# First v blocks ahead of the second q/k chunk, earlier masks, held sinks, later v: a reordering in a planned attention and MLP kernel

## The chip, the core and the metric

The kernel runs on one core of one Trainium2 chip. Its time is the device time in microseconds (us) of one execution; the figure quoted for a kernel is the median of several runs. TensorE does the matmuls, VectorE (DVE), ScalarE (ACT) and GpSimd (POOL) the elementwise work, and SyncE (SP) only issues transfers. POOL issues the loads that convert from float32 to bfloat16, SP the DMA transposes and the stores.

## What is computed

Sliding-window attention with sinks, then layer norm and an MLP with a residual. The reference, cut to what matters:

```python
# q, k, v: (4, 8, 768, 64); n_sink 4, window 128
scores = scale * np.matmul(q, k.transpose(0, 1, 3, 2))
is_sink = pos[None, :] < n_sink
rel = pos[:, None] - pos[None, :]
keep = is_sink | ((rel >= 0) & (rel < window))
a = softmax(np.where(keep, scores, -1e9))
x = matmul(a, v)                        # heads joined: (4, 768, 512)
xn = (x - mu) / np.sqrt(var + 1e-06) * g_ln
out = x + np.maximum(xn @ w_ch1, 0.0) @ w_ch2   # 512 -> 2048 -> 512
```

## The kernel before

**Tiles.** The 4 x 768 rows are 24 tiles of 128 rows, numbered t = 6b + r for row block r of batch b. A tile is attended by `scores` (L472), exp on ScalarE (L509), a mask, and `values` (L544). A block of 128 keys meets its own 128 queries and the next 128, so one set of scores is 64x128 by 64x256 matmuls (L498) in two halves of four heads, each half in one of two PSUM buffers `pw`. For the first four tiles the mask is added on TensorE (L494, from neg0 and neg1); for the others it is multiplied afterwards, on VectorE (L513, L519) or POOL (L521, L524). `values` multiplies by v with an extra column of ones (L565, L568), adds the sinks (L558, from row block 2 on), and empties the `pw` buffer on VectorE: reciprocal L590, product L592 (xt), statistics L598 and L601, centred and multiplied by g L606 (xn). xn is transposed on TensorE (L645), from tile 12 on by a DMA transpose (L635).

**Sinks.** Keys 0 to 3 of a batch reach every row. `sinks` (L426) makes masked copies of the sink keys (ks, L434, on VectorE, from the transposed k), spreads the sink values (L444 on TensorE, L449 on VectorE), multiplies all later queries by the sink keys (L457) and takes the exp (es, L462).

**MLP.** Tiles are in groups of 2, 2, 2, 4, 4, 4, 4, 2. `up` (L658) does 4 matmuls with w_ch1 (L666) and a relu on ScalarE or VectorE (L675, L677), 16 times per group; `down` (L685) does 16 matmuls with w_ch2 (L697) per tile, then L710 and the store L715. For the first three groups all ups come ahead of all downs. The reciprocal standard deviation of a group is made on POOL (L618 ve, L620 rs) from its tiles' statistics.

**Loads.** All loads of q, k, v and the weights are issued by POOL in one chain; at most eight are outstanding, as the trace shows. Batch 0's q and k come in two chunks of 384 rows (the first in two halves of heads), batch 1's in one (`load_runs`, L303), and both are transposed on TensorE (L386, `prep_runs`) and copied to qkt by ScalarE or VectorE (L182, L184). Batches 2 and 3 are loaded by row block (`load_qk`, L327) and transposed by DMA on SP (`prep`, L409). v is loaded by row block (`load_v`, L336).

**Order.** Nothing is scheduled at run time: each engine runs its own list in order. The list is made when the program is built. Every step is an `op` with its engines, an assumed cost, a key (its due time) and its dependencies. `Plan.emit` (L54) keeps a clock for each engine, takes the engine that can start first, and among the ops that could start there within a small slack the one of the lowest key. `LAT` (L37) is what is assumed between the end of an op and its use by another engine: 2.0 for a load, 0.7 for a DMA transpose. Ahead of each TensorE op before 26 us of that clock it puts dummy matmuls (`spin`, L192) into the gap it foresees (L104 to L109). The assumed costs therefore decide which instruction stands where, and a wait that was foreseen wrongly holds up all that stands behind it on its engine. The steps that the prediction follows are L434 on VectorE, the loads L312, L336 and L327 and the selects L242 and L244 on POOL, and L386, L494, L498, L558, L565, L666 and L697 on TensorE.

Of the kernel before, what the change touches and what calls it, by code (L numbers as in the profile page):

```python
# [31 lines left out]
class Plan:  # L32
# [10 lines left out]
    WARM = 26.0  # L43
    AHEAD = 2.5

    def __init__(self, spin):
        self.ops, self.spin = [], spin

    def op(self, engs, fn, deps=(), key=0.0, alloc=(), uses=()):
        o = Op(engs, fn, deps, key, alloc, uses)  # L50
        self.ops.append(o)
        return o

    def emit(self):  # L54
# [3 lines left out]
        def ready(o):  # L58

            r, held = 0.0, False  # L60
            for d in o.deps:
                if d.end is None:
                    return None, False

                r = max(r, d.end - (self.LAT[d.eng] - 0.03 if len(o.engs) == 1 and d.eng in o.engs else 0.0))
            n = {}
            for b in o.alloc:
                h = hist.get(b.pool, [])
                k = n[b.pool] = n.get(b.pool, -1) + 1
                if len(h) + k >= b.bufs:  # L70
                    for u in h[k - b.bufs].users:
                        if u.end is not None:
                            r = max(r, u.end)
                        elif b.pool == "pw":
                            held = True
                        else:
                            return None, False
            return (None if held else r), held

        trace = []  # L80
        while waiting:
# [7 lines left out]
            for o in waiting:  # L89
                r = at[o]  # L90
                if r is None:
                    continue
                if any(b.pool == "pw" for b in o.alloc) and any(o.key > k and max(r, free.get("PE", 0.0)) > a for k, a in pairs):
                    continue
                e, c = min(o.engs.items(), key=lambda x: max(r, free.get(x[0], 0.0)) + x[1] + (
                    self.SPARE.get(x[0], 0.0) if len(o.engs) > 1 else 0.0))
                s = max(r, free.get(e, 0.0))
# [6 lines left out]
            if e == "PE" and s < self.WARM:  # L104
                f = max(free.get(e, 0.0), 1.3)
                n = int((min(s, 5.0) - f) / 0.107) if f < 5.0 else 0
                n += int((s - max(f, 5.0) - 0.1) / 0.057) if s > 5.0 else 0
                for _ in range(n if s < 7.0 else n // 2):
                    self.spin()  # L109
            free[e] = s + c  # L110
            o.end, o.eng = s + c + self.LAT[e], e
            for b in o.alloc:
# [9 lines left out]
def kernel(  # L122
# [12 lines left out]
    nc = tc.nc  # L135
# [138 lines left out]
    ident_done = op({"POOL": 0.35}, const_ident, [begun], -499.5)  # L274
    half_masks = op({"POOL": 0.7}, const_masks, [begun], -488)
    masks_done = neg_done = op({"DVE": 0.8}, const_negs, [half_masks], -495)
    sinks_done = op({"POOL": 1.4}, const_sinks, [begun], -440)
# [24 lines left out]

    def load_runs(b, c, x, h0, h1, key):  # L303
        alloc = qn_buf(b, x)
# [9 lines left out]

        o = load(0.6 + 0.04 * (h1 - h0), (h1 - h0) * w * 256 / 390e3, go, key, (), alloc, [qb])
        for h in range(h0, h1):
            loaded[(b, c, x, h)] = o

    def load_qk(b, x, r, key, deps=()):
# [8 lines left out]

        o = load(0.9, 0.92, go, key, deps, alloc, [qb])
        prep(b, x, r, o, key)  # L330
# [3 lines left out]
    def load_v(b, r, key, deps=()):  # L334
# [4 lines left out]
        before = [vread[(b - 2, i)] for i in (r, r + 1) if (b - 2, i) in vread] + [vs_done.get(b - 2)]  # L339
        vcast[(b, r)] = load(0.9, 0.92, go, key, list(deps) + before)  # L340

# [59 lines left out]
    def prep(b, x, r, lo, key):  # L401
# [9 lines left out]
        o = op({"SP": 1.25}, go, [lo], key, alloc, [kb, qb])  # L411
        prepped[(b, r, x)] = op({"XD": 0.4}, None, [o], key, (), [kb, qb])

# [9 lines left out]

    sunk, esb = {}, {}

    def sinks(b, key):  # L426
# [36 lines left out]

        o1 = op({"DVE": 0.2}, mul_k, ready(b, range(HP), 0, NS, 0, 0) + [sunk.get(b - 2), sinks_done], key, (), [kb])
        ov = op({"PE": 0.22}, mm_v, [vcast[(b, 0)], sinks_done, ones_done], key, [vb])
# [3 lines left out]

    ebuf, edone = {}, {}  # L470

# [72 lines left out]
    def values(t, key):  # L544
# [89 lines left out]
        if t >= DMA_TILE:  # L634
            o = op({"SP": 1.25}, lambda _: nc.sync.dma_start_transpose(room(), xnb[t].t), [o], key, alloc,  # L635
                   [xnb[t], xtb[g]])
            turned[t] = op({"XD": 0.4}, None, [o], key, (), [xnb[t], xtb[g]])
            return
# [97 lines left out]

    gb_done = op({"PE": 1.0}, spread_g, [op({"SP": 5.2}, None, key=-1000)], -600, [gp])
    gb_done = op({"ACT": 0.6}, lambda _: nc.scalar.copy(gb, gp.t), [gb_done], -600, (), [gp])

    for half in range(2):  # L740
        for x in range(2):
            load_runs(0, 0, x, 4 * half, 4 * half + 4, -500 + half)
    for x in range(2):
        load_runs(0, 1, x, 0, H, -491 + x)
    for r in range(3):
        load_v(0, r, -486 + r)
    for c in range(4):
        load_w(1, c, -470 + 2 * c)
        if c < 3:
            load_v(0, 3 + c, -469 + 2 * c)  # L750
    for c in range(3):
        load_w(2, c, -440 + c)
    for x in range(2):
        load_runs(1, 0, x, 0, H, -436 + x)
    load_w(2, 3, -434)
# [3 lines left out]
    for b in range(B):  # L759
        k0 = bkey[b]  # L760
        if b == 0:
            for c in range(2):
                for hp in range(HP):
                    prep_runs(0, c, hp, k0 + (0.6 if c else -40) + 0.1 * hp)
                if c == 0:
# [19 lines left out]
        else:  # L785
# [3 lines left out]
            for r in range(RB):  # L789
                load_v(b, r, k0 - 50 + r)  # L790
        sinks(b, akey(RB * b + 2) - 6)
        for r in range(RB):
            attention(RB * b + r, akey(RB * b + r))

    for s, g in mlp_order:
# [48 lines left out]
```

## Time and profile before

| | |
|---|---|
| time, median of 13 runs | 237.33 us (236.5 to 243.31) |
| profiled execution: time | 237.33 us |
| profiled execution: span, mean granted clock | 235.6 us, 0.978 |
| TensorE busy | 224.0 us, of which up (L666) 88.5, down (L697) 57.9 + 31.7 |
| VectorE, ScalarE, POOL busy | 113.8, 116.2, 79.6 us |
| chain that ended last | TensorE 83%, DMA 6%, VectorE 5% |
| loads | 24.93 MB moved, mean 106 GB/s; batch 1's k: 768 KB, 20.9 us from issue to landing |
| DMA transposes of q and k (24) | 8.1 us from issue to landing |

How to read it. The span runs from the first to the last instruction of the profiled execution; the time has a little more around it. A row of the timeline gives the start, the duration, the engine, the line and the operation, output <- inputs, and in brackets how long the engine was idle before and what ended that. "xN" joins N instructions. A row of the windows gives for each engine the busy time in the stretch and the number of instructions, then the granted TensorE clock as a share of full speed, the DMA engines' share and GB/s. Releasers are inferred; where the engine named had long been done, it was something else, often a DMA.

### The profile page before, as it was taken

How to read it: one execution, taken by the hardware profiler on the slowest of the kernel's cores; microseconds unless marked ns; L12 is line 12 of the kernel's file. 1: busy time of each engine (PE TensorE's matmuls, PEld its weight loads, DVE VectorE, ACT ScalarE, POOL GpSimd, SP SyncE). 2: the span in 40 equal slices, each digit the busy share in tenths (PEclk: the TensorE clock that was granted, in tenths of full speed). 3: DMA queues.
4: the chain of work that ended last, by engine and by line, in shares of the span. 5: the costliest groups of instructions: out<-in, count | busy, mean ns of one | idle time of the engine just before them, and what ended most of it. 6: DMA issues, size and time to landing. Idle time of an engine off the chain costs nothing.

```text
span 235.6 us, 4404 instructions
## 1 busy us (share of the span) xinstructions
PE 224.0 (95%) x1808; PEld 123.3 (52%) x1808; DVE 113.8 (48%) x211; ACT 116.2 (49%) x188; POOL 79.6 (34%) x106
## 2 busy tenths in 40 slices
PE   8798999989879999999999999999999999999993
PEld 6344678876425455544555444454445554444851
DVE  1328578058476879856648445753007570021011
ACT  2467787879323553787123864316633147500820
POOL 7958663569716777530020300202004120000000
PEclk9679999999979999999999999999999999999999
DMA  6999999999999999999132101212002221012102
GB/s 70 152 180 191 199 206 205 200 157 154 127 154 163 168 207 156 181 159 168 58 93 88 22 3 24 93 67 67 0 1 69 90 67 25 0 45 89 47 0 89
DMA packets 83478, 24.93 MB, mean 106 GB/s; under 512 B 74241, under 2 KB 80385, under 8 KB 83458
## 3 DMA queue, kind: packets, MB, share of 16 engines
q0 software_dynamic: 60416, 13.64, 68.5%
q1 hardware_dynamic: 23040, 11.02, 22.6%
q8 instruction: 14, 0.23, 0.4%
q14 instruction: 6, 0.05, 0.1%
q10 hardware_dynamic: 2, 0.00, 0.0%
HBM read 27.27 MB, written 6.29 MB: 142 GB/s over the span
## 4 chain that ended last, share of the span: by engine, by line
PE 83%; DMA 6%; DVE 5%; ACT 2%; issue 1%; POOL 1%; SPq 0%; POOLq 0%; DVEq 0%; ACTq 0%
PE pm L697 35%; PE pm L666 32%; PE pw L498 5%; DMA qkt<-qkn 3%; PE pw L565 2%; DMA qkn<-in_k_dram 2%; PE pw L494 2%; PE pw L568 2%; PE pw L558 1%; DVE qkt L184 1%; DVE xt L592 1%; POOL qkn L312 1%; ACT e L509 1%; PE bank L645 1%; PE pm L386 1%
## 5 line engine op out<-in xcount | busy, mean ns | idle before, releaser
L666 PE MATMUL pm<-xnt,w1s 128*128 128x256 bf16 (+1 forms) x512 | 88.5, 326 | 0.0
L509 ACT ACTIVATE e<-pw 128x1024 bf16<-128x1024 f32 x44 | 43.7, 1024 | 49.5 <-PE pw L498 49.5
L666 PEld LDWEIGHTS <-w1s 128*128 128x128 bf16 x512 | 48.4, 98 | 33.3 <-issue 2.3
L697 PE MATMUL pm<-w2s,h1t 128*128 128x512 bf16 x256 | 57.9, 379 | 0.0
L710 DVE SCALAR_TENSOR_TENSOR ot<-pm,rs,xt 128x512 f32<-128x512 f32 x24 | 18.0, 748 | 64.2 <-PE pm L697 46.9
L675 ACT ACTIVATE h1t<-pm 128x512 bf16<-128x512 f32 x60 | 35.8, 597 | 21.9 <-PE pm L666 21.9
L697 PEld LDWEIGHTS <-h1t 128*128 128x128 bf16 x256 | 24.1, 98 | 28.2 <-issue 0.8
L697 PE MATMUL pm<-w2s,h1n 128*128 128x512 bf16 x128 | 31.7, 391 | 0.0
L675 ACT ACTIVATE h1n<-pm 128x256 bf16<-128x256 f32 x57 | 21.2, 389 | 17.6 <-PE pm L666 15.2
L336 POOL DMA_DIRECT2D vn<-in_v_dram x24 | 21.4, 896 | 4.7 <-DMA qkn<-in_q_dram 1.4
L521 POOL TENSOR_SCALAR_AFFINE_SELECT e<-e 128x512 bf16<-128x512 bf16 x7 | 4.5, 640 | 50.8 <-ACT e L509 50.8
L618 POOL TENSOR_SCALAR ve<-mv 128x2 f32<-128x2 f32 (+1 forms) x8 | 5.5, 683 | 46.6 <-DVE mv L601 46.4
L697 PEld LDWEIGHTS <-h1n 128*128 128x128 bf16 x128 | 11.9, 100 | 13.5 <-issue 2.9
L519 DVE TENSOR_TENSOR e<-e,mask 128x1024 bf16<-128x1024 bf16 x23 | 17.1, 748 | 3.7 <-ACT e L509 3.6
L606 DVE SCALAR_TENSOR_TENSOR xn<-xt,mv,gb 128x512 bf16<-128x512 bf16 x24 | 18.2, 762 | 0.8
L498 PE MATMUL pw<-qkt 64*128 64x256 bf16 (+1 forms) x192 | 15.8, 274 | 2.6 <-DVE xt L592 2.4
L598 DVE BATCH_NORM_STATS2 st<-xt 128x6 f32<-128x512 bf16 x24 | 16.7, 694 | 0.7
L592 DVE TENSOR_TENSOR xt<-pw,rc 128x512 bf16<-128x512 f32 x24 | 16.6, 691 | 0.8
L565 PE MATMUL pw<-vn,e 128*128 128x65 bf16 x192 | 15.8, 193 | 0.0
L565 PEld LDWEIGHTS <-e 128*128 128x128 bf16 x192 | 13.7, 97 | 2.6 <-issue 0.2
L498 PEld LDWEIGHTS <-qkt 64*128 64x128 bf16 x192 | 6.8, 95 | 15.0 <-issue 11.3
L568 PE MATMUL pw<-vn,e 128*128 128x65 bf16 x160 | 14.2, 193 | 0.0
(62 smaller groups left out, 168.1 us busy)
## 6 DMA issues: line engine op xcount, KB each, us to landing
out_dram<-ot SPq DMA_DIRECT2D x24, 256.0 KB, 2.2
vn<-in_v_dram POOLq DMA_DIRECT2D x24, 128.0 KB, 13.5
w1s<-in_moe_w_ch_dram POOLq DMA_DIRECT2D x4, 512.0 KB, 12.0
w2s<-in_moe_w_ch_dram POOLq DMA_DIRECT2D x4, 512.0 KB, 15.1
qkn<-in_q_dram POOLq DMA_DIRECT2D x12, 128.0 KB, 9.0
qkn<-in_k_dram POOLq DMA_DIRECT2D x12, 128.0 KB, 9.1
qkn<-in_q_dram POOLq DMA_DIRECT2D x1, 768.0 KB, 17.9
qkn<-in_k_dram POOLq DMA_DIRECT2D x1, 768.0 KB, 20.9
```

The source lines that it names most:

```text
L336: nc.gpsimd.dma_start(vn_buf[b % 2][:, r, :, 0:D], v[b, :, 128 * r:128 * (r + 1), :].rearrange("h p d -> p h d"))
L498: nc.tensor.matmul(pb.t[:, h2, i], lhsT=kb.t[64 * h2:64 * (h2 + 1), 1, hp, 128 * r:128 * (r + 1)], rhs=kb.t[64 * h2:64 * (h2 + 1), 0, hp, ...
L509: nc.scalar.activation(eb.t, pb.t, AF.Exp, scale=scale)
L519: nc.vector.tensor_tensor(ev, ev, mask1[:, 0:n].unsqueeze(1).to_broadcast([128, m, n]), op=ALU.mult)
L565: nc.tensor.matmul(pv[:, half, hh, :], lhsT=weights_of(t, half, i, h2, 0), rhs=vn[:, r, h, 0:D + 1], start=fresh and hh == 0, stop=(r == 0 ...
L568: nc.tensor.matmul(pv[:, half, hh, :], lhsT=weights_of(t - 1, half, i, h2, 128), rhs=vn[:, r - 1, h, 0:D + 1], start=False, stop=True, ski ...
L592: nc.vector.tensor_tensor(xb[t].t.rearrange("p (a h) d -> p a h d", a=2), pv[:, :, :, 0:D], rc[0].unsqueeze(3).to_broadcast([128, 2, 4, D] ...
L606: nc.vector.scalar_tensor_tensor(xnb[t].t, in0=xf, scalar=mvb[g][:, ti, 0:1], in1=gb, op0=ALU.subtract, op1=ALU.mult)
L666: nc.tensor.matmul(pb.t[:, 0:n], lhsT=w1s[:, j, 128 * ht:128 * (ht + 1)], rhs=xtb[g].t[:, j, 0:n], start=(j == 0), stop=(j == NDM - 1))
L675: nc.scalar.activation(hb.t[:, 0:n], pb.t[:, 0:n], AF.Relu)
L697: nc.tensor.matmul(pb.t, lhsT=h1b[(g, ht)].t[:, 128 * ti:128 * (ti + 1)], rhs=w2s[:, ht, :], start=(ht == 0), stop=(ht == NH1 - 1))
L710: nc.vector.scalar_tensor_tensor(ob.t, in0=pb.t, scalar=rsb[g][:, ti:ti + 1], in1=xb[t].t.rearrange("p h d -> p (h d)"), op0=ALU.mult, op1 ...
```

## The change

The order of POOL's load chain is changed: v0 and v1 of batch 0 go ahead of the second q/k chunk, and the two mask selects ahead of them. The matmul that spreads g (L735) is due later, and its copy may run on VectorE. Of the foreseen gaps after 7 us, four fifths instead of half are filled with dummy matmuls. Sinks of batches 1 to 3 are added after the second tile's attention with a later key, and their first step is made to depend on the first tile's masked scores in the plan. The v of batches 2 and 3 depend in the plan on the batch's last DMA transpose. The assumed landing of a DMA transpose is 6.0 us later for q and k, 3.0 for xn of tiles up to 17; other assumed costs of loads and masks are changed. Both choices of engine and the whole order after these points are made anew by the planner. The program's instructions are otherwise the same. The diff:

```diff
@@ -42,12 +42,14 @@
 
     WARM = 26.0
     AHEAD = 2.5
+    EARLY = 16.0
 
     def __init__(self, spin):
         self.ops, self.spin = [], spin
 
-    def op(self, engs, fn, deps=(), key=0.0, alloc=(), uses=()):
+    def op(self, engs, fn, deps=(), key=0.0, alloc=(), uses=(), lat=0.0):
         o = Op(engs, fn, deps, key, alloc, uses)
+        o.lat = lat
         self.ops.append(o)
         return o
 
@@ -62,7 +64,7 @@
                 if d.end is None:
                     return None, False
 
-                r = max(r, d.end - (self.LAT[d.eng] - 0.03 if len(o.engs) == 1 and d.eng in o.engs else 0.0))
+                r = max(r, d.end - (self.LAT[d.eng] + d.lat - 0.03 if len(o.engs) == 1 and d.eng in o.engs else 0.0))
             n = {}
             for b in o.alloc:
                 h = hist.get(b.pool, [])
@@ -93,7 +95,7 @@
                 if any(b.pool == "pw" for b in o.alloc) and any(o.key > k and max(r, free.get("PE", 0.0)) > a for k, a in pairs):
                     continue
                 e, c = min(o.engs.items(), key=lambda x: max(r, free.get(x[0], 0.0)) + x[1] + (
-                    self.SPARE.get(x[0], 0.0) if len(o.engs) > 1 else 0.0))
+                    self.SPARE.get(x[0], 0.0) if len(o.engs) > 1 and r > self.EARLY else 0.0))
                 s = max(r, free.get(e, 0.0))
                 cand.append((s, e, o, c))
                 first[e] = min(first.get(e, 1e9), s)
@@ -105,10 +107,10 @@
                 f = max(free.get(e, 0.0), 1.3)
                 n = int((min(s, 5.0) - f) / 0.107) if f < 5.0 else 0
                 n += int((s - max(f, 5.0) - 0.1) / 0.057) if s > 5.0 else 0
-                for _ in range(n if s < 7.0 else n // 2):
+                for _ in range(n if s < 7.0 else 4 * n // 5):
                     self.spin()
             free[e] = s + c
-            o.end, o.eng = s + c + self.LAT[e], e
+            o.end, o.eng = s + c + self.LAT[e] + o.lat, e
             for b in o.alloc:
                 hist.setdefault(b.pool, []).append(b)
             waiting.remove(o)
@@ -272,8 +274,8 @@
     begun = op({"POOL": 0.7}, None, key=-1000)
     ones_done = op({"DVE": 2.0}, None, key=-1000)
     ident_done = op({"POOL": 0.35}, const_ident, [begun], -499.5)
-    half_masks = op({"POOL": 0.7}, const_masks, [begun], -488)
-    masks_done = neg_done = op({"DVE": 0.8}, const_negs, [half_masks], -495)
+    half_masks = op({"POOL": 0.6}, const_masks, [begun], -492)
+    masks_done = neg_done = op({"DVE": 1.3}, const_negs, [half_masks], -495)
     sinks_done = op({"POOL": 1.4}, const_sinks, [begun], -440)
 
 
@@ -300,7 +302,7 @@
         qn[(b, x)] = Buf("qkn", 4)
         return [qn[(b, x)]]
 
-    def load_runs(b, c, x, h0, h1, key):
+    def load_runs(b, c, x, h0, h1, took, key):
         alloc = qn_buf(b, x)
         qb = qn[(b, x)]
         w = S // CHUNKS[b]
@@ -312,7 +314,7 @@
             nc.gpsimd.dma_start(dst[:, c, h0:h1], (q, k)[x][b, h0:h1, c * w:(c + 1) * w, :]
                                 .rearrange("h (p r) d -> p h (r d)", p=128))
 
-        o = load(0.6 + 0.04 * (h1 - h0), (h1 - h0) * w * 256 / 390e3, go, key, (), alloc, [qb])
+        o = load(0.9 if h1 - h0 == H else 0.77, took, go, key, (), alloc, [qb])
         for h in range(h0, h1):
             loaded[(b, c, x, h)] = o
 
@@ -326,7 +328,7 @@
             dst = qb.t.rearrange("p (r h d) -> p r h d", r=RB, h=H)
             nc.gpsimd.dma_start(dst[:, r], (q, k)[x][b, :, 128 * r:128 * (r + 1), :].rearrange("h p d -> p h d"))
 
-        o = load(0.9, 0.92, go, key, deps, alloc, [qb])
+        o = load(0.9, 0.9, go, key, deps, alloc, [qb])
         prep(b, x, r, o, key)
 
     vcast, vread, vs_done = {}, {}, {}
@@ -337,7 +339,7 @@
                                 v[b, :, 128 * r:128 * (r + 1), :].rearrange("h p d -> p h d"))
 
         before = [vread[(b - 2, i)] for i in (r, r + 1) if (b - 2, i) in vread] + [vs_done.get(b - 2)]
-        vcast[(b, r)] = load(0.9, 0.92, go, key, list(deps) + before)
+        vcast[(b, r)] = load(0.9, 0.85, go, key, list(deps) + before)
 
     w1s = consts.tile([128, NDM, DH], BF16)
     w2s = consts.tile([128, NH1, DM], BF16)
@@ -409,7 +411,7 @@
             nc.sync.dma_start_transpose(kb.t[:, x, :, 128 * r:128 * (r + 1)], qb.t[:, H * D * r:H * D * (r + 1)])
 
         o = op({"SP": 1.25}, go, [lo], key, alloc, [kb, qb])
-        prepped[(b, r, x)] = op({"XD": 0.4}, None, [o], key, (), [kb, qb])
+        prepped[(b, r, x)] = op({"XD": 0.4}, None, [o], key, (), [kb, qb], 6.0)
 
     def ready(b, hps, klo, khi, qlo, qhi):
 
@@ -421,7 +423,7 @@
         return [prepped[(b, r, x)] for x in range(2) for r in range(RB)
                 if 128 * r < ends[x][1] and 128 * (r + 1) > ends[x][0]]
 
-    sunk, esb = {}, {}
+    sunk, esb, edone = {}, {}, {}
 
     def sinks(b, key):
 
@@ -461,13 +463,13 @@
             eb.t = espool.tile([128, S - 256], BF16, name="es")
             nc.scalar.activation(eb.t, pb.t, AF.Exp, scale=scale)
 
-        o1 = op({"DVE": 0.2}, mul_k, ready(b, range(HP), 0, NS, 0, 0) + [sunk.get(b - 2), sinks_done], key, (), [kb])
+        o1 = op({"DVE": 0.2}, mul_k, ready(b, range(HP), 0, NS, 0, 0) + [sunk.get(b - 2), sinks_done, edone.get((RB * b, 0)) if b else None], key, (), [kb])
         ov = op({"PE": 0.22}, mm_v, [vcast[(b, 0)], sinks_done, ones_done], key, [vb])
         vs_done[b] = op({"DVE": 0.7}, mul_v, [ov, vread.get((b - 2, RB - 1))], key, (), [vb])
         o2 = op({"PE": 0.4}, mm, [o1] + ready(b, range(HP), 0, 0, 256, S), key, [pb], [kb])
         sunk[b] = op({"ACT": 0.6}, ex, [o2], key, [eb], [pb])
 
-    ebuf, edone = {}, {}
+    ebuf = {}
 
     def scores(t, halves, key):
 
@@ -634,7 +636,7 @@
         if t >= DMA_TILE:
             o = op({"SP": 1.25}, lambda _: nc.sync.dma_start_transpose(room(), xnb[t].t), [o], key, alloc,
                    [xnb[t], xtb[g]])
-            turned[t] = op({"XD": 0.4}, None, [o], key, (), [xnb[t], xtb[g]])
+            turned[t] = op({"XD": 0.4}, None, [o], key, (), [xnb[t], xtb[g]], 3.0 if t < 18 else 0.0)
             return
         pt = Buf("pt", 1)
 
@@ -734,24 +736,23 @@
         gp.t = ps_m.tile([128, 512], FP32, name="pm")
         nc.tensor.matmul(gp.t, lhsT=ones, rhs=grow, start=True, stop=True)
 
-    gb_done = op({"PE": 1.0}, spread_g, [op({"SP": 5.2}, None, key=-1000)], -600, [gp])
-    gb_done = op({"ACT": 0.6}, lambda _: nc.scalar.copy(gb, gp.t), [gb_done], -600, (), [gp])
+    gb_done = op({"PE": 1.0}, spread_g, [op({"SP": 7.0}, None, key=-1000)], bkey[0] - 1, [gp])
+    gb_done = op({"ACT": 0.6, "DVE": 0.65}, lambda e: copy(e, gb, gp.t), [gb_done], bkey[0] - 1, (), [gp])
 
     for half in range(2):
         for x in range(2):
-            load_runs(0, 0, x, 4 * half, 4 * half + 4, -500 + half)
+            load_runs(0, 0, x, 4 * half, 4 * half + 4, ((1.5, 1.0), (1.6, 1.1))[half][x], -500 + half)
+    for r in range(2):
+        load_v(0, r, -491 + r)
     for x in range(2):
-        load_runs(0, 1, x, 0, H, -491 + x)
-    for r in range(3):
-        load_v(0, r, -486 + r)
+        load_runs(0, 1, x, 0, H, (2.8, 2.04)[x], -488 + x)
     for c in range(4):
         load_w(1, c, -470 + 2 * c)
-        if c < 3:
-            load_v(0, 3 + c, -469 + 2 * c)
+        load_v(0, 2 + c, -469 + 2 * c)
     for c in range(3):
         load_w(2, c, -440 + c)
     for x in range(2):
-        load_runs(1, 0, x, 0, H, -436 + x)
+        load_runs(1, 0, x, 0, H, 3.85, -436 + x)
     load_w(2, 3, -434)
     for r in range(RB):
         load_v(1, r, -430 + r)
@@ -761,7 +762,7 @@
         if b == 0:
             for c in range(2):
                 for hp in range(HP):
-                    prep_runs(0, c, hp, k0 + (0.6 if c else -40) + 0.1 * hp)
+                    prep_runs(0, c, hp, k0 + (0.6 + 0.1 * hp if c else 0.15 if hp > 1 else -40))
                 if c == 0:
                     for n in range(4):
                         scores(n % 2, (n // 2,), k0 + 0.1 * n)
@@ -787,10 +788,11 @@
                 for x in range(2):
                     load_qk(b, x, r, k0 - 60 + r, [prepped.get((b - 1, RB - 1, 1))])
             for r in range(RB):
-                load_v(b, r, k0 - 50 + r)
-        sinks(b, akey(RB * b + 2) - 6)
+                load_v(b, r, k0 - 50 + r, [prepped[(b, RB - 1, 1)]])
         for r in range(RB):
             attention(RB * b + r, akey(RB * b + r))
+            if r == 1:
+                sinks(b, akey(RB * b + 2) - 1)
 
     for s, g in mlp_order:
         if s == "u" and g < NB0:
```

## The prediction

> **What bounds the kernel now.** I read the page first: busy shares, the slices, the chain that ended last.
>
> ```profile
> span 235.6 us, 4404 instructions
> PE 224.0 (95%) x1808; PEld 123.3 (52%) x1808; DVE 113.8 (48%) x211; ACT 116.2 (49%) x188; POOL 79.6 (34%) x106
> ...
> PE   8798999989879999999999999999999999999993
> ...
> PEclk9679999999979999999999999999999999999999
> DMA  6999999999999999999132101212002221012102
> ```
>
> A slice is 5.9 us. TensorE is full from slice 12 (about 70 us) to the end, so nothing can be won there but by issuing fewer matmuls, and the change takes no real one away. Two stretches are weak: slices 1 and 2, and slices 10 and 11. In both the granted clock drops too. The DMA row is full up to slice 18, which matters below. Next I asked for the work of the second weak stretch, by windows:
>
> ```profile
> core 0: us, PE busy (x) PEld busy (x) DVE busy (x) ACT busy (x) POOL busy (x), PEclk, DMA share, GB/s
> 61.86:66.50 4.64, 2.22 (x19) 0.80 (x16) 1.03 (x4) 1.02 (x1) 2.66 (x4) 0.97 2.07 138
> 66.50:70.05 3.55, 3.55 (x13) 1.25 (x14) 3.37 (x6) 1.02 (x1) 0.00 (x0) 0.56 1.74 155
> 70.05:231.70 161.65, 161.65 (x1097) 81.08 (x1095) 75.24 (x130) 71.48 (x110) 32.28 (x40) 1.00 0.59 81
> ```
>
> TensorE idles 2.4 us, then works 3.5 us at a clock of 0.56, then never waits again (161.65 of 161.65). TensorE's waits name the releaser, and VectorE's timeline shows what stood before it:
>
> ```profile
> PE pw L498 <- DVE xt L592: 2.4, 1, 2.4
> ```
>
> ```profile
> 60.70 0.69 DVE L449 TENSOR_TENSOR vs<-pw,smask 128x520 bf16<-128x520 f32 x1
> 65.41 0.19 DVE L434 TENSOR_TENSOR ks<-qkt,hmask 128x32 bf16<-128x32 bf16 x1 [4.02 <-DMA qkt<-qkn]
> 65.52 0.20 DVE L590 RECIPROCAL rc<-pw 128x8 f32<-128x8 f32 x1
> 65.75 0.69 DVE L592 TENSOR_TENSOR xt<-pw,rc 128x512 bf16<-128x512 f32 x1
> ```
>
> L434 makes the masked sink keys of batch 2. Nobody needs them before 91 us (L457 there), but the instruction waits 4.02 us for a DMA transpose at the head of VectorE's queue. Behind it stand L590 and L592 of tile 7; L592 empties the PSUM buffer that the second half of tile 8's scores (L498) wants. Last, the first stretch and its way to the next stage:
>
> ```profile
> 16.56 0.42 PE L565 MATMUL pw<-vn,e 128*128 128x65 bf16 x8
> ...
> 18.77 0.60 PE L494 MATMUL pw<-mask,ident 128*128 128x512 bf16 x2
> ...
> 24.96 0.28 PE L558 MATMUL pw<-vs,es 128*128 128x260 bf16 x1
> ```
>
> ```profile
> 25.10 0.88 POOL L312 DMA_DIRECT2D qkn<-in_k_dram  x1
> ...
> 46.52 0.87 POOL L327 DMA_DIRECT2D qkn<-in_q_dram  x1 [2.65 <-PE pm L666]
> ```
>
> ```profile
> 46.94 1.53 PE L386 MATMUL pw<-ident,qkn 128*64 128x128 bf16 x48
> ```
>
> The k of batch 1 (768 KB, 20.9 us to landing in the page's DMA list) lands at 25.10 + 20.9 = 46.0. The load eight places later starts at 46.52 after a wait that the trace puts down to L666; I read it as a wait for that landing, since the v at 13.61 likewise waited for the q eight loads ahead of it. So k can be used from about 46.4, and TensorE starts batch 1's transposes at 46.94: only half a microsecond of slack. **Up to 46 us the start is bound by the load queue, whatever TensorE does.**
>
> **The change, part by part.**
>
> *Sinks held.* In the changed order L434 of batch 2 stands after VectorE's masks of tiles 12 and 13, some 40 places later, when the transposes have long landed. Saved: from 61.86 (end of tile 7's values) to the scores at 71.23 before, TensorE did 20 down matmuls (L697), one set of scores, one transpose of xn. At the full rate, by the chain's own pieces, that is 20 x 0.216 + 0.54 + 0.22 = 5.1 us; it took 9.4. The difference, 4.25 us, is 2.42 of waiting, 1.37 for eight L697 at the low clock (3.10 against 1.73), and 0.46 on the split scores. What is late next: L590 of tile 7 then follows L449 at once, xt is done about a microsecond after the values, and the 1.7 us of down matmuls ahead of the scores hide it.
>
> [...] The row says 0.56 right after that wait, and I take the row: 4.25.
>
> *First v ahead, masks ahead, first scores ahead.* POOL's two mask selects (0.33 + 0.32) move from 6.67 to 4.93, VectorE's five mask instructions from 7.28–8.83 to about 5.6–7.1, so that tile 0's first scores can follow the first transposes: about 8.5 against 10.23. v0 and v1 go out at 5.6 instead of 7.2, and land near 11 instead of 16.2, so values(0) can run near 13.4 against 16.56. But the second chunk's q and k, issued at 4.92 and 5.79 before, go out at 7.3 and 8.2 behind two v's. Those v's landed 0.8 and 0.9 apart, so k lands 1.7 later, 17.1 for 15.4; with the best loading rate of the first slices it could be as early as 15.5. On TensorE the chunk's first transposes now stand ahead of values(1), so both wait for it. By hand: transposes 17.0, first mask of tile 2 about 20.0 (18.77 before), but the sinks are made by then, and L558 comes at about 24.7 (24.96 before) with one up group (4 L666) more done. On the changed order 132 up matmuls stand ahead of batch 1's transposes, 140 before; with the four already done that is 12 fewer from L558 on, 1.3 us at 0.108. Arrival: 46.94 – 0.3 – 1.3 = 45.3, and then TensorE waits for k at 46.4. The same 20 loads stand ahead of that k, and the queue is full, so it does not move. The k half of the first transposes starts at 46.4 instead of 47.14 (0.75 won), and the 8 up matmuls left over come later (0.87 lost): together 0.1 lost. Bounds: k lands 1.2 us earlier if the stretch at 8–10 us, where the loads ran slowest, is better now; or 0.7 later.
>
> *More spinning.* 84 dummy matmuls instead of 54, 30 x 0.057 = 1.7 us. They fill waits for DMA and ScalarE ahead of 25 us, which the load queue covers; without that cover up to 1.7.
>
> *g spread after the transposes; a second engine for its copy.* One L735 of 1.05 us and one copy of 0.6, both under the same cover: 0.
>
> *Between 52 and 62 us.* The new order puts both exps of tile 7 in front of the sinks' exp and of the relus, so L444 waits for a PSUM buffer and the next up matmuls for a relu. With 1.02 per exp and 0.39 per relu I get 1.0 us of TensorE idle, where before 61.86 – 52.76 = 9.1 us held about 0.45. Cost 0.55; bounds 0 and 1.2.
>
> *v of batch 2 behind the transposes.* Six issues of 0.9 move on POOL past one window select pair and the rstd pair (ve, rs) of tiles 6–9, which waits for tile 9's statistics: from 59.26 to about 74. Queued behind them are the q and k of batch 3; these go from 73.94 to about 80, still with 25 us before they are used. v0 is wanted by values(12) near 84, so it may take 9.7 us. The nearest rows, q and k loads issued at 73.94 to 83.0, took 8.8 to 9.7 us with six v's still ahead; those issued at 49–54 took 6.0 to 6.8. I take 8: no wait. Below nothing: the batch's transposes (8.1 us each) run without v beside them, but nothing waits for them then.
>
> Sum: –4.25 + 0.1 + 0.55 = –3.6 us. Profiled execution: span 235.6, time 237.33, 1.73 outside the span; it equals the median of 13 runs. 237.33 – 3.6 = **233.7 us**.
>
> **Rivals.**
> A. The start does pass through: k of batch 1 lands 1.2 us earlier. For: the slow stretch at 8–10 us. Against: the same bytes. 232.5. Chance 0.15.
> B. Waiting for k near 46 lowers the clock once more. For: in 5.2–8.6, idle for a third of the time, it went down. Against: I count 0.9 us idle. About 1.5 of work at half rate: 235.2. Chance 0.16.
> C. It does not do what it says: VectorE or TensorE waits in the same place for something else (a transpose, a mask on POOL), and most of the 4.25 comes back: 236.7. Chance 0.06.
> D. Slower. v0 of batch 2, now behind tile 9's statistics on POOL, comes too late for values(12). It decides at a latency of 9.7 us. For: the page's median for v is 13.5 us. Against: those had other loads queued ahead, this one has none. At 13.5: 3.8 waiting and 1.4 of lost clock, 233.7 + 5.2 = 238.9. Chance 0.09.
> The forecast itself: 0.54.
>
> **How the numbers follow.** The forecast's own terms (±0.7 for k, 0–1.2 for 52–62 us) give 232.7 to 234.9. With A and B inside: 232.3 to 236.0, leaving out C and D. 0.5% is 1.2 us, about what a measurement of this kernel can tell from no change. Faster by more (below 236.1): 0.84; within: 0.07; slower: 0.09.
>
> **What would show it.** VectorE's L434 of batch 2 without a DMA wait and after 75 us; no 2.4 us wait of L498 on L592; the clock at 1.0 through 60–75. TensorE waiting for a qkn load just ahead of 46.4, the transposes starting there. The second chunk's k landing near 17 and a TensorE gap ahead of it. v of batch 2 issued near 74, values(12) without a wait. I am wrong if batch 1's transposes start much before 46, or if a new wait of over 1 us shows between 60 and 90.

## The result and the profile after

The changed kernel takes **235.53 us** (median of 11 runs, 234.26 to 236.12) against 237.5 us before: ratio 0.9911, 95% interval 0.9887 to 0.9935, so 2.1 us or 0.9% less. A second set of runs (e4) gave 235.1 us and 0.9913 (0.9889 to 0.9937). Forecast were 233.7 us and a range of 232.3 to 236.0: the sign and the range held, the point was 1.8 us too low. Ratios leave disturbed executions out; in the table below this concerns e11, where three of six remain, and e7, where twelve of fourteen do.

The profiled execution took 234.57 us, with a span of 232.9 us (235.6 before). First its slices on the page, TensorE's busy tenths and the granted clock:

```profile
PE   8967999989899999999999999999999999999993
PEclk9999999999999999999999999999999999999999
```

The dip of slice 11 (65 to 71 us; 7 in both rows before) has gone, and so have the low clocks at 8 to 15 us. Slice 10 stays at 8, now for another reason (below), and slices 2 and 3 are less busy than before (6 and 7, before 9 and 8). Line numbers of the changed kernel are two higher than before (L436 is the old L434, L594 the old L592). Next the windows: of before, and then of the changed kernel (columns as in the prediction: TensorE's busy time, its weight loads, VectorE, ScalarE, POOL, the clock).

```profile
52.00:62.00 10.00, 9.79 (x103) 6.67 (x101) 8.15 (x16) 7.91 (x16) 9.61 (x12) 1.00 2.83 145
```

```profile
52.00:62.00 10.00, 8.54 (x97) 6.28 (x94) 7.91 (x18) 7.76 (x14) 7.00 (x8) 1.00 2.29 130
62.00:67.00 5.00, 5.00 (x38) 2.32 (x36) 3.59 (x7) 1.94 (x2) 1.23 (x2) 1.00 1.85 154
```

From 62 us on TensorE is never idle before the end, at full clock. But in the ten microseconds ahead of that it now idles 1.46 us, where before it idled 0.21. VectorE's timeline shows that the instruction which stood there has left the place:

```profile
60.67 0.69 DVE L451 TENSOR_TENSOR vs<-pw,smask 128x520 bf16<-128x520 f32 x1
61.57 0.21 DVE L592 RECIPROCAL rc<-pw 128x8 f32<-128x8 f32 x1 [0.21 <-PE pw L570]
61.81 0.69 DVE L594 TENSOR_TENSOR xt<-pw,rc 128x512 bf16<-128x512 f32 x1
```

The reciprocal of tile 7 now waits 0.21 us for its own values instead of standing 4 us behind L434. The key copy of batch 2 comes at 94.56 us, right behind tile 13's masks, without a wait. TensorE's longest waits are now at the start and in the stretch just named:

```profile
PE pm L388 <- DMA qkn<-in_k_dram: 1.7, 1, 1.7
PE bank L194 <- ACT xnt L184: 1.5, 2, 0.9
PE bank L647 <- DVE xn L608: 1.4, 2, 1.0
```

### The profile page after: what moved, and what is told of

The parts are those of the page before. It is cut to its first block, busy times and chain, and to the rows that moved or that the text cites. A ratio compares the mean times of both kernels' runs of the same rounds, so it can differ in the third digit from the quotient of the medians.

```text
span 232.9 us, 4451 instructions
## 1 busy us (share of the span) xinstructions
PE 221.3 (95%) x1838; PEld 123.8 (53%) x1838; DVE 114.8 (49%) x213; ACT 115.4 (50%) x186; POOL 78.0 (34%) x105
## 4 chain that ended last, share of the span: by engine, by line
PE 83%; DVE 7%; DMA 4%; POOL 3%; ACT 2%; issue 1%; POOLq 0%
PE pm L699 36%; PE pm L668 32%; PE pw L500 4%; DMA qkn<-in_k_dram 4%; PE pw L567 2%; PE pw L570 2%; POOL qkn L314 2%; DVE xn L608 1%; PE pw L560 1%; ACT qkt L184 1%; PE bank L647 1%; DVE st L600 1%; DVE xt L594 1%; DVE qkt L186 1%; POOL vn L338 1%; PE pw L388 1%
## 5 line engine op out<-in xcount | busy, mean ns | idle before, releaser
L668 PE MATMUL pm<-xnt,w1s 128*128 128x256 bf16 (+1 forms) x512 | 88.7, 326 | 0.1
L668 PEld LDWEIGHTS <-w1s 128*128 128x128 bf16 x512 | 48.4, 98 | 33.2 <-issue 2.4
L677 ACT ACTIVATE h1t<-pm 128x512 bf16<-128x512 f32 x59 | 35.2, 597 | 21.7 <-PE pm L668 21.7
L699 PE MATMUL pm<-w2s,h1n 128*128 128x512 bf16 x128 | 30.0, 379 | 0.0
L677 ACT ACTIVATE h1n<-pm 128x256 bf16<-128x256 f32 x56 | 21.0, 386 | 17.5 <-PE pm L668 15.2
L620 POOL TENSOR_SCALAR ve<-mv 128x2 f32<-128x2 f32 (+1 forms) x8 | 4.8, 600 | 56.8 <-DVE mv L603 56.7
L608 DVE SCALAR_TENSOR_TENSOR xn<-xt,mv,gb 128x512 bf16<-128x512 bf16 x24 | 18.7, 783 | 2.6 <-DMA xnt<-xn 1.9
L523 POOL TENSOR_SCALAR_AFFINE_SELECT e<-e 128x512 bf16<-128x512 bf16 (+1 forms) x7 | 4.9, 700 | 44.1 <-ACT e L511 44.1
L521 DVE TENSOR_TENSOR e<-e,mask 128x1024 bf16<-128x1024 bf16 x23 | 16.2, 710 | 4.9 <-ACT e L511 4.8
L594 DVE TENSOR_TENSOR xt<-pw,rc 128x512 bf16<-128x512 f32 x24 | 16.6, 692 | 0.8
L500 PE MATMUL pw<-qkt 64*128 64x256 bf16 (+1 forms) x192 | 14.7, 263 | 0.1
```

Of the source, the lines that this page charges most:

```text
L500: nc.tensor.matmul(pb.t[:, h2, i], lhsT=kb.t[64 * h2:64 * (h2 + 1), 1, hp, 128 * r:128 * (r + 1)], rhs=kb.t[64 * h2:64 * (h2 + 1), 0, hp, ...
L594: nc.vector.tensor_tensor(xb[t].t.rearrange("p (a h) d -> p a h d", a=2), pv[:, :, :, 0:D], rc[0].unsqueeze(3).to_broadcast([128, 2, 4, D] ...
L608: nc.vector.scalar_tensor_tensor(xnb[t].t, in0=xf, scalar=mvb[g][:, ti, 0:1], in1=gb, op0=ALU.subtract, op1=ALU.mult)
L668: nc.tensor.matmul(pb.t[:, 0:n], lhsT=w1s[:, j, 128 * ht:128 * (ht + 1)], rhs=xtb[g].t[:, j, 0:n], start=(j == 0), stop=(j == NDM - 1))
L677: nc.scalar.activation(hb.t[:, 0:n], pb.t[:, 0:n], AF.Relu)
L699: nc.tensor.matmul(pb.t, lhsT=h1b[(g, ht)].t[:, 128 * ti:128 * (ti + 1)], rhs=w2s[:, ht, :], start=(ht == 0), stop=(ht == NH1 - 1))
```

## Experiments

My theory at first was the prediction's own sum: holding the sinks is the gain, and the rest is small change. Its rivals: the later v carries the gain (e7, e8); another wait takes the place of the one removed (e1); the front is what wins or loses (e2, e10).

| run | what it is | median us (range) | ratio to before, 95% |
|---|---|---|---|
| e1 | before + sinks of batches 2, 3 held | 240.64 (239.31–241.70) | 1.0152 (1.0116–1.0188) |
| e2 | before + the front | 241.32 (240.47–243.65) | 1.0200 (1.0158–1.0243) |
| e3 | e1 and e2 | 241.28 (240.73–243.01) | 1.0196 (1.0159–1.0233) |
| e4 | the changed kernel | 235.10 (233.69–236.92) | 0.9913 (0.9889–0.9937) |
| e5 | e1 + one mask on VectorE | 233.06 (232.45–233.25) | 0.9835 (0.9798–0.9873) |
| e6 | e1 + later v | 232.71 (232.46–233.16) | 0.9824 (0.9791–0.9858) |
| e7 | before + later v | 236.86 (234.97–238.99) | 0.9973 (0.9940–1.0007) |
| e8 | changed, without later v | 235.65 (234.62–236.65) | 0.9937 (0.9911–0.9962) |
| e9 | changed, batch 1's sinks as before | 233.19 (232.78–235.64) | 0.9847 (0.9798–0.9895) |
| e10 | changed, front as before | 233.70 (233.25–234.19) | 0.9855 (0.9823–0.9887) |
| e11 | changed, without both | 236.57 (233.02–239.46) | 0.9866 (0.9810–0.9922) |
| e12 | e6 + nine dummy matmuls | 233.27 (232.53–233.55) | 0.9836 (0.9800–0.9872) |

**e1: the hold alone.** TensorE's, ScalarE's, POOL's and SyncE's orders are those of before; on VectorE only L434 of batches 2 and 3 moves.

```diff
-        o1 = op({"DVE": 0.2}, mul_k, ... + [sunk.get(b - 2), sinks_done], key, (), [kb])
+        o1 = op({"DVE": 0.2}, mul_k, ... + [sunk.get(b - 2), sinks_done, edone.get((RB * b, 0)) if b > 1 else None], key, (), [kb])
...
-        sinks(b, akey(RB * b + 2) - 6)
+        if b == 1:
+            sinks(b, akey(RB * b + 2) - 6)
...
+            if r == 1 and b > 1:
+                sinks(b, akey(RB * b + 2) - 6)
```

> The kernel before with one thing moved: on VectorE the masked sink keys of batches 2 and 3 stand after the batch's first masked scores. TensorE's, ScalarE's, POOL's and SP's orders are the same as before. My theory (the wait of that instruction for a DMA transpose held up VectorE, then TensorE for 2.4 us, and the clock went to half for a window): 4.25 us less, 233.2; TensorE has no wait for the product that empties the PSUM buffer near 64 us and the clock stays at 1.0 from 60 to 75. Rival, a gap of 2.4 us costs no clock: 2.4 less, 235.0. Rival, another wait takes its place: less than 1 us, 236.5 or more.

It came out 3.6 us **slower**. The stall at 62 us is gone as expected (TensorE busy 13.00 of 13.00 in 62 to 75 us, clock 1.00; in before it was at 0.50 from 66.23 to 69.64 us). But there is a new wait, shown first by TensorE's waits, then on POOL's timeline:

```profile
PE pw L565 <- POOL e L521: 5.1, 1, 5.1
```

```profile
88.55 1.77 POOL L336 DMA_DIRECT2D vn<-in_v_dram  x2
...
96.75 0.87 POOL L336 DMA_DIRECT2D vn<-in_v_dram  x1 [0.73 <-DMA qkn<-in_k_dram]
97.63 0.65 POOL L521 TENSOR_SCALAR_AFFINE_SELECT e<-e 128x512 bf16<-128x512 bf16 x1
```

The second half of tile 13 is masked on POOL, and that mask stands behind six issues of v of batch 3, which themselves wait for earlier loads to land. TensorE, now 4 us earlier, stands ready for values(13) at 93.2 and gets it at 98.3; then its clock falls (0.69 in 99 to 103 us). The trace of before had the same mask just in time, its second select ending at 97.5, with values(13) at 97.8 without a wait:

```profile
95.82 0.66 POOL L521 TENSOR_SCALAR_AFFINE_SELECT e<-e 128x512 bf16<-128x512 bf16 x1
```

By the profiled execution, the fastest of the six, the span is 2.0 us longer than before. So the next bound lay 0.3 us behind the first, in another queue and 30 us later. My sum could not stand on the hold alone.

**e2, e3: the front alone, and with the hold.** The front is the order of POOL's first loads, the masks, the first scores, the spread of g and the dummies, with the costs the plan takes for them:

```diff
-    half_masks = op({"POOL": 0.7}, const_masks, [begun], -488)
+    half_masks = op({"POOL": 0.6}, const_masks, [begun], -492)
...
+    for r in range(2):
+        load_v(0, r, -491 + r)
...
-        load_runs(0, 1, x, 0, H, -491 + x)
-    for r in range(3):
-        load_v(0, r, -486 + r)
+        load_runs(0, 1, x, 0, H, (2.8, 2.04)[x], -488 + x)
```

> The kernel before with the front of the change alone: first v blocks and masks ahead, spread of g later, more dummy matmuls, the assumed costs of loads and masks; no held sinks, no later v, no longer assumed landing. My theory (the start is bound by the load queue up to batch 1's k, and eight up matmuls are left for later): 0.1 lost to 0.9 won, about 237; the 4 us wait of the sink keys of batch 2 is still there. Rival, what the changed kernel won it won at the front: 235.5.

> The front as in the run of the front alone, and the held sinks of batches 2 and 3 alone; the v loads and the assumed landings as before, batch 1's sinks where they were. My theory: the sum of the two, 232.9 to 233.3, so two us less than the changed kernel, which loses them between 52 and 62 us. Rival, the later v and the assumed landings are needed for the gain: no better than the changed kernel, 235.5.

Both are slower by 4.7 us. In e2 the stall near 64 us is still there (1.9 us), TensorE waits 2.2 us for tile 13's mask, and the clock is at a half from 17.6 to 21.0 us, behind a wait of 1.7 us for the second chunk's k, and again from 92.7 to 96.1 us, behind the mask. In e3, with the hold, the wait for the mask has grown (lines are one higher here):

```profile
PE pw L566 <- POOL e L522: 6.6, 1, 6.6
```

**e4: the changed kernel again**, on the same chip as these.

> The changed kernel once more, to see where the clock falls in the executions that take longer. 235.5; span 232.7 with the clock at 1.0 or 233.8 at 0.99. My theory: one window of half clock after the wait for the second chunk's k near 14 to 16 us or after the waits at 57 to 60 us.

As it was: 0.9913. Its profile is of an execution at full clock, so it does not show where the longer ones lose theirs; e8 shows one such place. Hold and front together lose 4.7 us and the whole change wins 2.1, so something in what remained, the later v, the assumed landings and the other handling of the sinks, had to be what lets the gain through.

**e5, e6: two ways round the mask.** In e5 one mask moves from POOL to VectorE, which is idle from 92.4 to 99.4 us in e1; the planner also shifts a load and a step of the reciprocal standard deviation by a few places on POOL. In e6 only POOL's order differs from e1.

```diff
-                    o = op({"POOL": 1.28, "DVE": 0.69}, window, [o, masks_done], key, (), [eb])
+                    o = op({"DVE": 0.69} if t == 13 else {"POOL": 1.28, "DVE": 0.69}, window, [o, masks_done], key, (), [eb])
```

```diff
-                load_v(b, r, k0 - 50 + r)
+                load_v(b, r, k0 - 50 + r, [prepped[(b, RB - 1, 1)]])
```

> The kernel of e1 (sinks of batches 2 and 3 held, nothing else changed) with one mask moved: the second half of tile 13 is masked on VectorE instead of POOL. TensorE's, ScalarE's and SyncE's orders are those of e1. Theory (what eats the gain of the hold is only that mask standing behind POOL's loads, which wait for free load slots): VectorE is idle from 92.4 to 99.4 us in e1, so the mask is done near 93, the wait of 5.1 us of values(13) and the low clock after it go, 240.6 - 5.1 - 1.7 = 233.8 us. Rival (the later loads themselves are what is late: q, k and v of batch 3): values(13) runs early but another wait follows between 95 and 115 us, 236 us or more.

> The kernel of e1 with the later v edit alone added; only POOL's order differs from e1. Theory (the v edit is what lets the gain through): with the v of batch 2 out of the way of the transposes, POOL's loads no longer wait for slots, q and k of batch 3 are issued by about 92 and tile 13's mask follows at once, so at most 1 us of the 5.1 us wait is left: 234 to 235 us. Rival (the v edit does nothing for POOL's queue, loads wait for slots as before): the mask stays near 97, 239 to 241 us. Rival D of the prediction: v of batch 2 now comes too late for values(12): a wait there of 2 us or more, 237 or more.

One moved mask takes 240.64 to 233.06 us, a little more than the theory said (233.8), and no other wait follows:

```profile
90.00:100.00 10.00, 10.00 (x70) 4.96 (x69) 7.41 (x13) 7.97 (x13) 7.68 (x10) 1.00 1.69 172
```

The later v does as much, 232.71, the lowest median of this study and by the ratios 2.1 us under the changed kernel. POOL's timeline of e6:

```profile
88.41 0.88 POOL L327 DMA_DIRECT2D qkn<-in_k_dram  x1
...
91.31 1.07 POOL L521 TENSOR_SCALAR_AFFINE_SELECT e<-e 128x512 bf16<-128x512 bf16 x1
...
97.64 5.36 POOL L336 DMA_DIRECT2D vn<-in_v_dram  x6
```

The reason I gave for e6 was wrong in part. POOL's loads of q and k still wait for earlier ones to land, and the last of them goes out at 88.41, in e1 at 87.68. What differs is that the six v of batch 3 now stand behind the mask instead of ahead of it.

**e7, e8: the later v alone, and everything but it.** e7 is before with the second diff above; e8 is the changed kernel with that diff reversed.

> The kernel before with the later v edit alone; only POOL's order differs. Theory: the 62 to 66 us stall stays, because L434 still stands ahead of tile 7's normalisation and still waits for a transpose; POOL's chain gets shorter where nothing waited for it. Within 0.5% of before: 236.5 to 238.5 us. Rival (the transposes land sooner when no v is loaded beside them, so L434's 4.0 us wait shrinks by 2 us or more): 233.5 to 235.5 us, and then the v edit would carry the gain without the hold.

> The changed kernel with the v of batches 2 and 3 back in their old place; TensorE's and ScalarE's orders are those of the changed kernel, and tile 13 is masked on VectorE in both. Theory (POOL's blocked queue hurts only through tile 13's mask): no wait of over 1 us comes back near 93, 234.5 to 236 us. Rival (later v is needed for more than that mask): slot waits on POOL between 65 and 95 us delay the masks of tile 8, the rstd or batch 3's transposes, and TensorE waits 2 us or more for one of them, 237.5 to 241 us.

e7 is within what can be told from no change: L434 waits as long without v loads beside the transposes. First VectorE, then the windows of e7:

```profile
65.06 0.19 DVE L434 TENSOR_TENSOR ks<-qkt,hmask 128x32 bf16<-128x32 bf16 x1 [4.05 <-DMA qkt<-qkn]
```

```profile
62.00:67.00 5.00, 2.54 (x18) 0.92 (x17) 1.83 (x6) 1.43 (x2) 0.00 (x0) 1.00 1.89 133
67.00:75.00 8.00, 7.97 (x75) 4.19 (x74) 6.16 (x12) 3.14 (x4) 3.86 (x6) 1.00 1.09 146
```

The stall is the same, 2.46 us, yet here the clock stays at 1.00 behind it, where in the trace of before it fell to 0.56. e8 can't be told from the changed kernel either (0.9937 against 0.9911, the intervals overlap), since there tile 13's second mask is on VectorE anyway, and TensorE does not wait near it:

```profile
90.00:100.00 10.00, 10.00 (x77) 4.69 (x75) 8.28 (x16) 6.02 (x10) 4.65 (x6) 1.00 1.86 168
```

So the hold and *one* of two ways round the mask make the gain; the changed kernel has both.

Its profile shows one more thing. TensorE's order at the start is that of the changed kernel, and both wait 1.75 us for the k of the second chunk. The windows just behind that wait, e8 first, then the changed kernel:

```profile
17.04:20.35 3.31, 3.31 (x58) 3.05 (x58) 1.72 (x5) 1.76 (x3) 1.43 (x2) 0.50 1.54 193
```

```profile
16.42:19.80 3.38, 2.63 (x64) 2.20 (x65) 2.26 (x5) 2.73 (x5) 1.51 (x2) 1.00 1.54 193
```

In e8 the clock is at a half from 16.96 to 20.37 us, in the other execution it is not. TensorE's order and its wait are the same, so something that differs between executions decides (the next section comes back to it). Of the 31 of the changed kernel (with e4), 15 had a mean clock of 0.997 or more and a mean span of 232.84 us; 16 had 0.989 to 0.993, and 234.12. Both profiled ones are of the first kind, so that the second kind loses its clock at this place is inferred from e8 and not shown.

**e9, e10, e11: what parts the changed kernel from e6.** e9 makes batch 1's sinks early again, e10 has the front of before, e11 both.

```diff
-        o1 = op(... edone.get((RB * b, 0)) if b else None], key, (), [kb])
+        o1 = op(... edone.get((RB * b, 0)) if b > 1 else None], key, (), [kb])
...
+        if b == 1:
+            sinks(b, akey(RB * b + 2) - 6)
...
-            if r == 1:
+            if r == 1 and b > 1:
```

> The changed kernel with the sinks of batch 1 made early, as before; those of batches 2 and 3 stay held. Theory (the 1.45 us that TensorE idles in 52 to 62 us come from holding batch 1's sinks: both exps of tile 7 then stand ahead of the relus, and tile 6's normalised rows come later than TensorE asks for them): the idle time there falls to about 0.2, as in e6, 1.2 us less than the changed kernel: 234.2 to 234.5 us. Rival (the idle time comes from the order of the front, with eight more up matmuls left over): it stays, 235.2 to 236 us. If holding batch 1 is all that parts the changed kernel from e6: 232.5 to 233.2.

> The changed kernel with the front of before (loads of v, masks, first scores, spread of g and dummy matmuls as before); held sinks, later v and the assumed landings stay. Theory (the front wins nothing: its wait for the second chunk's k, 1.7 us, leaves eight more up matmuls after batch 1's transposes, 0.87 us, against an arrival only 0.25 us earlier): about 0.6 us less than the changed kernel, 234.6 to 235.1 us, batch 1's transposes at 46.3. Rival (the front wins what was hoped for at the start and this shows without it): 236 us or more. Second rival (the front alone parts the changed kernel from e6): 232.5 to 233.2.

> The changed kernel with the front of before and batch 1's sinks as before: what is left of the change is the held sinks of batches 2 and 3, the later v and the longer assumed landing of DMA transposes. TensorE's order up to 90 us is that of e6. Theory (the two costs add up and the assumed landings move nothing that is waited for): as e6, 232.4 to 233.2 us. Rival (the assumed landings cost or win something beyond 90 us, where they reorder masks and relus): 1 us or more away from e6.

e9 is 1.5 us faster than the changed kernel by the ratios, about 1 us below what I expected by the times. Its idle time in 52 to 62 us is 0.22, as in e6. Up to 52 us its profile is the changed kernel's (batch 1's transposes at 46.06, tile 6's scores at 51.88), and then:

```profile
59.37 1.03 PE L699 MATMUL pm<-w2s,h1n 128*128 128x512 bf16 x4
60.24 0.39 PE L647 MATMUL bank<-ident,xn 128*128 128x128 bf16 x4
```

The first down matmul stands at 59.37, in the changed kernel at 61.37, and the transpose of xn does not wait. e10 is 1.3 us faster by the ratios, but its profile misses what I expected of it: batch 1's transposes start at 46.92, not 46.3.

```profile
46.92 1.53 PE L388 MATMUL pw<-ident,qkn 128*64 128x128 bf16 x48
```

It is the longest of the six executions, with a wait of 0.82 us for the second chunk's k. The changed kernel's 46.06 and the eight matmuls that it still has to do then (0.87 us) come to 46.93, so between these two executions the front costs nothing. By executions of full clock alone the mean span is 231.95 us in e10 and 232.84 in the changed kernel, so the front costs about 0.9 us there. The rest of the 1.3 agrees with the half-clock stretch, which no profile of e10 or e6 shows at that place. The two costs don't add up exactly (1.3 and 1.5 against 2.1 to e6), which the intervals of about 0.9 us either way allow.

e11 gave no size, since its times spread over 6 us. The profiled execution (238.59 us), one of the long ones, shows where it lost time; there is no profile of a short one beside it. SyncE's queue issues ten transposes of q and k in a row from 92.31 to 110.57 us, then those of xn, and VectorE waits for one of these to free a buffer:

```profile
118.93 0.75 DVE L608 SCALAR_TENSOR_TENSOR xn<-xt,mv,gb 128x512 bf16<-128x512 bf16 x1 [7.15 <-DMA xnt<-xn]
```

The masks of the next tile stand behind it, and TensorE loses 3.5 us. In e6 the same twelve transposes of batch 3 stand ahead of those of xn, but the last of them is issued by 103.8, and that L606 ran at 112.23 without a wait. Their loads go out from 74.44 us on in e6 and from 81.96 in e11, where the reciprocal standard deviation of tiles 6 to 9 stands ahead of them on POOL. Whether the longer assumed landings put it there, or the sinks' later key in e11, was not tried; the assumed landings were never changed by themselves.

**e12: more dummies.** One line, `4 * n // 5` for `n // 2`, on e6.

> The kernel of e6 (sinks of batches 2 and 3 held, later v) with nine more dummy matmuls in gaps between 13 and 25 us; all other orders are those of e6. Theory (they fill waits that the load queue covers): 232.5 to 233 us, as e6, batch 1's transposes at 46.3. Rival 1 (they stand in the way of work that is ready): later by up to 9 x 0.057 = 0.5 us, 233.2. Rival 2 (the clock falls in some executions in these gaps and the dummies prevent it): the highest times go, median 232.3 or less, mean clock 1.0 in all executions.

232.53 to 233.55 us, two of six at a mean clock of 0.985: the dummies did not keep the clock up in all executions, and won nothing.

## Why the prediction came out as it did

- **Sinks held, –4.25: right in the changed kernel, but not by itself.** From 61.37 to 66.65 us the work from the end of tile 7's values to the next scores took 5.28 us, all busy, against 9.37 before: 4.09 saved. What the step left out is *what is late next* beyond tile 7. It looked at L590 and the matmuls ahead of the scores, and not at the places 30 us later that were met only because TensorE was late: tile 13's mask on POOL. e1 gives all of the gain back there, and by the ratios 3.6 us more. That the changed kernel escapes rests on where the planner put a mask and on the later v, and **the prediction costed the later v at 0 without seeing that it clears the way**. In the changed kernel itself 0 holds (e8). The forecast had not looked there, so that its sum held on this point was luck.
- **The size of the 4.25.** 1.37 of it was a clock that fell in the profiled execution. e7 has the same stall without it. The saving that does not hang on the clock is 2.42 + 0.46 = 2.9 us: e7's executions of full clock had a mean span of 233.8, those of e5 and e6 230.9. The medians of e5 and e6 (–3.9 and –4.2) hold some of the clock as well.
- **52 to 62 us, +0.55: mis-sized; 1.25 more idle in the windows.** L444 waiting for a buffer was right (0.32 us at 57.5). The term missed that the transpose of tile 6's xn would come 1.00 us too early for VectorE. The cause is the hold of batch 1 (e9): tile 6's normalisation begins 0.8 us later (L592 at 57.49, in e9 at 56.72), and the up matmuls that are left stand behind the waiting transpose in TensorE's list (L668 at 60.44).
- **Front, +0.1: right in the balance, wrong in what bounds it.** Batch 1's transposes started at 46.06 (foreseen 46.4), 0.88 us earlier than before, and the eight matmuls left over took 0.87 back. But no wait for batch 1's k showed: it landed at 45.3, and TensorE arrived with its own work. The load queue is not the bound there. Second, the start of the transposes differs between executions of one order: with the front of before it lies between 45.91 and 46.94 us in eight profiles, 46.43 in the mean, and the profile of before is the latest. With the new front it is 46.19 in the mean of three profiles whose clock does not fall at 17 us, and 47.15 in the mean of three where it does (e2, e3, e8). With the 0.87 us still to do, the front so *loses* about 0.6 us without that fall, and 1.6 with it; in the changed kernel about half of the executions have a lower mean clock, at 1.3 us each.
- **Where the 1.8 us went:** 0.9 is in the profiled execution, whose span fell by 2.7 us for 3.6: 0.7 of it is the mis-sized term of 52 to 62 us (1.25 for 0.55), 0.16 the hold (4.09 for 4.25). Another 0.7 (16 of 31 executions at 1.28) is the lower clock of about half of the executions; the rest is within the spread of the medians. Rival B was of this kind, but at 46 us instead of 17, and the row of before that showed a clock falling after 2.4 us idle was the one that should have been laid beside the new wait that I foresaw there. The two bounds that the prediction named, ±0.7 and 0 to 1.2, add to 232.4 to 235.1 and not to 232.7 to 234.9; the range that was forecast covers both.
- **Spinning, g and later v at 0:** e12 and e8 give no sign against it for spinning and the later v; g was not tried by itself. Rivals A, C and D did not come. For D: the v of batch 2 went out at 76.3 to 81.6 us and landed within 6 us.

A wait of TensorE of 1.75 us (e8 and the changed kernel) and one of 2.42 and 2.46 us (before and e7) each had the clock fall behind them in one execution and not in the other. The changes of the granted clock within one execution lie whole multiples of 3.41 us apart: 8.20, 15.03, 66.23 and 69.64 us in before, 17.60, 21.01, 92.69 and 96.10 in e2. So the time of an execution can be laid out in stretches of 3.41 us from one of its changes. Here are those around the wait at 64 us, of before and then of e7, whose clock changes at 232.46, fifty such stretches after 61.80:

```profile
62.82:66.23 3.41, 1.26 (x9) 0.32 (x7) 0.79 (x3) 1.02 (x1) 1.75 (x2) 1.00 1.73 138
66.23:69.64 3.41, 3.14 (x11) 1.09 (x12) 3.34 (x7) 1.02 (x1) 0.00 (x0) 0.50 1.66 156
```

```profile
61.80:65.21 3.41, 1.90 (x12) 0.60 (x9) 0.14 (x2) 1.02 (x1) 0.00 (x0) 1.00 2.10 128
65.21:68.62 3.41, 2.43 (x16) 1.03 (x17) 3.31 (x8) 1.02 (x1) 0.00 (x0) 1.00 1.50 146
```

In before nearly all of the wait lies in one stretch, in which TensorE is busy for 1.26 us, and the next one has half the clock. In e7 two stretches share the same wait, with 1.90 and 2.43 us, and the clock stays. The wait at 17 us is alike: 1.44 us in e8's stretch ahead of the fall (13.55 to 16.96 us), 2.34 and 2.33 in the two of the changed kernel (11.93 to 18.75 us, laid out from its change at 233.79). In the profiles of before and of the changed kernel, up to 225 us, one more full-clock stretch was followed by a fall: that of 4.79 to 8.20 us in before, with TensorE busy for 2.68 us. Five with 2.33 to 2.59 us were not, so that fall stays open. In these two pairs of executions, then, where the wait lies in the stretches goes with whether it costs clock; no run moved a wait on purpose, and why the clock changes at these times was not shown.

## What to carry to other kernels

When a wait is removed, follow the engine that becomes earlier down every queue it will meet, and list what was met only just in time: here a mask 0.3 us ahead of its use, on another engine and 30 us later, took back the whole gain, and moving that one instruction released it. Test an edit made of several parts part by part: two of these parts cost about 1.3 and 1.5 us under a sum that looked right, and a version without them (e6) had the lowest median. A TensorE wait of about 2 us is to be priced with the clock as a chance, not as a certainty: behind waits of 1.75 us and of 2.42 to 2.46 us it fell to 0.50 here in one execution and stayed at 1.00 in another.

## What the hardware showed that I had not expected

- The same order of TensorE with the same wait (1.75 us at the start, 2.42 to 2.46 us at 64 us) had the clock at a half for 3.41 us behind it in some executions and at 1.0 in others. What parts them in these traces is whether one stretch of 3.41 us, laid out from the execution's own clock changes, holds most of the wait (TensorE busy for 1.26 us in before, 1.44 in e8) or two share it (1.90 and 2.43 us in e7, 2.34 and 2.33 in the changed kernel).
- Loads of 128 KB landed much later here among others. The v of batches 2 and 3, issued between 55 and 100 us of the kernel before with transposes and q/k loads in flight, took a median of 15.2 us to land, and 15.1 in e1; the v of batch 2 in the changed kernel, issued behind the transposes, 4.7 us. The transposes gained little from it: the median of those issued between 55 and 100 us is 8.0 us in before, 7.9 in the changed kernel and 7.2 in e6.
